# Chunked retention and two MLPs on one core: heads placed by the steps' length, six half tiles under way, value products of two heads in alternation

## Chip, core and metric

One core of a Trainium2 chip runs the whole program. The metric is the device time of one execution in microseconds (us). Three runs of the kernel before gave 1224.64, 1226.80 and 1226.89 us; their median is 1226.8 us.

## The reference, cut to what matters

Queries, keys and values are (4 batches, 8 heads, 768 positions, 64) in f32. A retention layer keeps a 64 x 64 state per batch and head; its output, laid out as 3072 tokens of 512, goes through two MLPs (512 to 2048 to 512) with different activations.

```python
gamma = 1.0 - 2.0 ** (-5.0 - np.arange(H, dtype=np.float32))
for t in range(S):
    state = gamma[None, :, None, None] * state + np.einsum('bhd,bhe->bhde', k[:, :, t], v[:, :, t])
    y[:, :, t] = scale * np.einsum('bhd,bhde->bhe', q[:, :, t], state)
x = y.transpose(0, 2, 1, 3).reshape(B * S, H * D)
h = x @ w_in;  x = np.maximum(0.01 * h, h) @ w_out          # first MLP
h = np.maximum(x @ w2_in, 0.0);  out = (h * h) @ w2_out     # second MLP
```

## The kernel before

**Retention.** The sequence is cut into chunks of 256, so there are 12 units (chunk, batch), the four batches of a chunk in a row. A unit has four pairs of heads; a pair's two heads lie in partitions 0 to 63 and 64 to 127. That makes 48 pairs, numbered 0 to 47 in this order, and 96 heads. For a head, `scores` multiplies keys by queries into PSUM (two blocks: the causal lower part of a 256 x 256 matrix), `soften` multiplies by the mask table on VectorE (L186, the mask product), and `values` multiplies by the values. After the second head of a pair, `outer` updates the state (L231) and `combine` writes the pair's part of the token matrix. `prep_pair` scales queries and values by decay tables first (L121, L122).

The first four units (`WHOLE = 4`, pairs 0 to 15) have no earlier state and are computed in plain f32: these are the unsplit pairs. Their scores contract over 64 partitions (L168, L169), and their value products write 64 output partitions, of the upper or lower half by head (L202, L203). An f32 product appears in the trace as two records. All later heads, the split ones, run as sums of products of f32r operands (a high part and a remainder): L176, L209, L215, with more work for VectorE and ScalarE (L135 to L159, L191, L192, L259, L260).

**MLPs.** The 3072 tokens are six blocks of 512; layer and block give 12 values of n, each with 16 steps, one per 128 columns of the hidden dimension. A step's first half (`emit_in`, L376 or L386) gives the hidden columns in one PSUM bank, `activate` applies the activation (L400, L401), and its second half (`emit_out`, L423 or L446) adds to four accumulator banks. Block 0 of the first layer is cut further: its first `HS = 5` steps take only the first 256 tokens, in plain f32, so that they can start when unit 0 alone is done; eleven steps of full length follow, then the five missing halves:

```python
steps += [(0, j, 0, C) for j in range(HS)]
steps += [(0, j, 0, T) for j in range(HS, NJ)]
steps += [(0, j, C, T) for j in range(HS)]
```

So steps 0 to 4 and 16 to 20 have half the length, steps 5 to 15 the full one, and from step 21 (n = 1) on all are full. From step 5 on weights, activations and tokens are split in f32r parts (`split_w`, L348, L349; `split_x`, L362 to L365).

**Weights** come from memory as 512 KB half tiles, in an 8-byte format that ScalarE and VectorE turn into f32 (`convert`, L303 to L309; VectorE's part is three instructions). `load_half` issues the transfer of the next one, and `convert` calls it again for each half tile used up, so the number under way stays what the start set: three, and one more after the first conversion. Up to step 13 the first layer's weights are converted, two steps ahead of their use (`AHEAD`); the second layer's come from step 80 on (`conv2`).

**Order.** The main loop runs over the steps: the next step's first half, then the heads that `place` put at this step (`head_at`), then this step's second half, then conversions. `place(k)` gives the step for head 8 + k; heads 0 to 7 stand before the loop. Before, heads 8 to 15 all stand at step 0, heads 16 to 31 spread over steps 0 to 13, and then one head stands at each of the steps 14 to 77. The code's order is not that of the engines: when the program is built, a planner orders each engine's instructions by the code's order and by modelled times. `keep_in_program_order` pins an instruction behind the one traced before it on its engine.

PSUM has eight banks: four for the accumulators, three for tag "h" (scores, hidden columns, outer products), one for the values' result y. All loads are issued on SyncE (SP) in one queue.

Of the kernel before, what the change touches and what calls it, by code (L numbers as in the profile page):

```python
# [9 lines left out]
F32 = mybir.dt.float32  # L10
# [7 lines left out]
P = 128  # L18
C = 256
# [23 lines left out]
def retention_then_two_mlps(  # L43
# [150 lines left out]
    def values(hu):  # L194
        u, p, h = hu
        if h == 0:
            y_ps[u, p] = ps_a.tile([P, 2, C], F32, tag="y", name="y")
        if u < WHOLE:
            qs, k, vs = prep[u, p]
            pm = p_sb.pop(hu)  # L200
            y = y_ps[u, p][64 * h:64 * h + 64, 0]
            nc.tensor.matmul(out=y, lhsT=vs[:, 0, h], rhs=pm[:, 128:384], start=True, stop=False)  # L202
            nc.tensor.matmul(out=y[:, P:2 * P], lhsT=vs[:, 1, h], rhs=pm[:, 0:128], start=False, stop=True)  # L203
            return
        q2, kh, kl, v2, vs, w2 = prep[u, p]
        y = y_ps[u, p][:, h]
        start = True
        if w2 is not None:
            nc.tensor.matmul(out=y, lhsT=w2[:, h].rearrange("p a e -> p (a e)"), rhs=q2[h], start=True, stop=False)  # L209
            start = False  # L210
        t = p_sb.pop(hu)
        for n in range(2):
            for sb in range(2):
                c, o = (P, 0) if sb else (0, P)
                nc.tensor.matmul(  # L215
                    out=y[:, c:C], lhsT=v2[:, sb, h].rearrange("p a e -> p (a e)"), rhs=t[:, n, o:o + C - c],
                    start=start, stop=n == 1 and sb == 1,
                )
                start = False

    def outer(up):

# [45 lines left out]
    def load_half():  # L268
        m = n_loaded[0]
        if m < len(halves):  # L270
            lay, j, half = halves[m]
            if lay == 0 and half == 0:
                early_stage[0] = slot(4 + j % 2, [P, 2, DM], U64, "sg")
            if lay == 0:
                t = early_stage[0][:, half]
            elif m % 3 == 2:
                t = a_p.tile([P, DM], U64, tag="r", name="sg", bufs=1)
            else:
                t = stage_p.tile([P, DM], U64, tag="sg", name="sg")
            stage[m] = t  # L280
            nc.sync.dma_start(out=t, in_=w[lay, j, half])
            n_loaded[0] += 1
# [184 lines left out]
    def place(k):  # L467

        if k < 8:
            return k * (HS - LEAD + 1) // 8  # L470
        k -= 8
        a, b = max(HS - LEAD + 1, 0), last_step[0] - LEAD
        if k < 16:
            return a + k * (b - a) // 16
        return b + (k - 16)

    def loads_to(n):
        while n_pairs[0] < min(n, len(ups)):
# [30 lines left out]
                outer(hu[:2])  # L509
            combine(hu[:2])  # L510

    nc.sync.dma_start(out=vt, in_=vtab)
    loads_to(1)
    nc.sync.dma_start(out=qt[:, 0], in_=qtab[:, 0])
    nc.sync.dma_start(out=mk, in_=mask)
    loads_to(2)
    nc.sync.dma_start(out=qt[:, 1:4], in_=qtab[:, 1:4])
    nc.sync.dma_start(out=gt, in_=gtab)
    loads_to(4)
    load_half()  # L520
    load_half()
    load_half()
    first_acc = ps_acc.tile([P, 4, T], F32, tag="acc", name="first_acc")
    for k in range(8):
        hu = hus[k]
        preps_to(k // 2 + 1)
        scores(hu)
        soften(hu)
        values(hu)
        after(hu)  # L530
    loads_to(6)
    need_x(0)
    converted_to(1)
# [9 lines left out]
    for i in range(N):  # L543
# [4 lines left out]
            activate(i + 1)  # L548
        for hu in head_at.get(i, []):
            preps_to(ups.index(hu[:2]) + 1)  # L550
            scores(hu)
            soften(hu)
            values(hu)
            after(hu)
            loads_to(n_prep[0] + 1)
        if i + 1 < N:
# [79 lines left out]
```

## Time and profile before

| | |
|---|---|
| median of three runs | 1226.8 us |
| the profiled execution | 1227.78 us |
| its span in the profile | 1225.8 us |
| TensorE (PE) busy | 1197.4 us, 98% |
| VectorE (DVE) busy | 864.8 us, 71% |
| ScalarE (ACT) busy | 694.8 us, 57% |
| mean granted TensorE clock | 0.995 |
| first matmul starts | 5.50 us |

A busy share is the time in which an engine had an instruction under way; a matmul's record is longer than its turn on the array, as the next one starts before it ends, so turns are read from one start to the next. The chain of work that ended last lies to 90% on TensorE.

### The profile page before, as it was taken

Reading aid. Unit: us, or ns where it says so; the run is one execution under the profiler, and the core shown is the slowest. Engines: PE = TensorE matmul, PEld = TensorE weight load, DVE = VectorE, ACT = ScalarE, POOL = GpSimd, SP = SyncE. Lnnn points to the kernel's source line nnn. Section 1 sums busy time; section 2 is a strip of 40 time slices with the busy share of each in tenths; the row PEclk is TensorE's granted clock in tenths of the full one; section 3 lists DMA queues with packets and bytes.
Section 4 is the critical chain, followed back from the end, with each engine's and each line's share of the span. In section 5 each row is a group of like instructions: output and inputs, shape, how many; then the busy total and the mean of one; then the engine's idle time right before and its main releaser. Section 6 shows DMA issues by size and latency. Waiting matters only on the chain.

```text
span 1225.8 us, 15223 instructions
## 1 busy us (share of the span) xinstructions
PE 1197.4 (98%) x5660; PEld 984.1 (80%) x5660; DVE 864.8 (71%) x1621; ACT 694.8 (57%) x1382; POOL 0.2 (0%) x4
## 2 busy tenths in 40 slices
PE   6799989999999999999999999999999999999998
PEld 4577788888888888888888788888888888888886
DVE  5888589889888888986699955645645555555553
ACT  4666476667666776775477744544534444444443
POOL 0000000000000000000000000000000000000000
PEclk9999999999999999999999999999999999999999
DMA  8664011111111111111045300000000000000000
GB/s 311 232 223 159 18 47 48 58 43 49 60 35 35 45 43 35 41 46 35 18 145 175 128 1 1 35 1 1 35 1 1 35 1 1 35 1 1 35 1 34
DMA packets 22825, 68.81 MB, mean 56 GB/s; under 512 B 2784, under 2 KB 5088, under 8 KB 22752
## 3 DMA queue, kind: packets, MB, share of 16 engines
q1 hardware_dynamic: 22752, 67.85, 16.6%
q8 instruction: 44, 0.72, 0.2%
q14 instruction: 29, 0.24, 0.1%
HBM read 61.55 MB, written 6.29 MB: 55 GB/s over the span
## 4 chain that ended last, share of the span: by engine, by line
PE 90%; DMA 4%; DVE 3%; ACT 2%; issue 1%; SPq 0%; ACTq 0%; DVEq 0%
PE acc L446 40%; PE h L386 40%; DMA sg<-w 3%; PE sc L176 2%; PE y L215 2%; PE y L202 1%; PE sp L231 1%; PE h L376 1%; PE y L209 1%; PE sc L169 1%; PE sc L168 1%; PE acc L423 1%; ACT w L303 1%; DMA gt<-gtab 1%; DVE w L309 0%
## 5 line engine op out<-in xcount | busy, mean ns | idle before, releaser
L386 PE MATMUL h<-xh,wih 128*128 128x512 f32 (+1 forms) x768 | 300.3, 391 | 0.2 <-DVE g L401 0.2
L386 PE MATMUL h<-xl,wih 128*128 128x512 f32 (+1 forms) x768 | 297.8, 388 | 0.9 <-DVE xl L365 0.9
L386 PE MATMUL h<-xh,wil 128*128 128x512 f32 (+1 forms) x768 | 298.5, 389 | 0.0
L349 DVE TENSOR_TENSOR wol<-w,woh 128x512 fp32r<-128x512 f32 x192 | 132.4, 690 | 145.5 <-ACT woh L348 144.4
L348 ACT CAST woh<-w 128x512 fp32r<-128x512 f32 x192 | 119.6, 623 | 181.0 <-PE acc L446 180.0
L386 PEld LDWEIGHTS h<-xl,wih 128*128 128x128 f32 x768 | 144.5, 188 | 30.9 <-DVE xl L365 1.7
L386 PEld LDWEIGHTS h<-xh,wih 128*128 128x128 f32 x768 | 144.5, 188 | 30.7 <-issue 1.2
L386 PEld LDWEIGHTS h<-xh,wil 128*128 128x128 f32 x768 | 144.6, 188 | 29.2 <-DVE wil L349 1.7
L411 DVE TENSOR_TENSOR gl<-g,gh 128x512 fp32r<-128x512 f32 (+1 forms) x192 | 130.8, 681 | 27.9 <-PE acc L446 12.6
L410 ACT CAST gh<-g 128x512 fp32r<-128x512 f32 (+1 forms) x192 | 118.4, 616 | 46.9 <-DVE g L404 26.8
L349 DVE TENSOR_TENSOR wil<-w,wih 128x512 fp32r<-128x512 f32 x192 | 131.4, 684 | 7.4 <-ACT wih L348 7.1
L348 ACT CAST wih<-w 128x512 fp32r<-128x512 f32 x192 | 118.0, 615 | 16.9 <-PE h L386 16.5
L446 PE MATMUL acc<-gh,woh 128*128 128x512 f32 (+1 forms) x388 | 108.8, 393 | 0.0
L404 DVE SCALAR_TENSOR_TENSOR g<-h,g 128x512 f32<-128x512 f32 x96 | 66.3, 690 | 58.8 <-ACT g L403 57.9
L446 PE MATMUL acc<-gh,wol 128*128 128x512 f32 (+1 forms) x388 | 106.2, 385 | 0.0
L446 PE MATMUL acc<-gl,woh 128*128 128x512 f32 (+1 forms) x388 | 105.7, 384 | 0.0
L446 PE MATMUL acc<-woh,gh 128*128 128x512 f32 x384 | 105.6, 389 | 0.0
L446 PE MATMUL acc<-woh,gl 128*128 128x512 f32 x384 | 105.6, 389 | 0.0
L446 PE MATMUL acc<-wol,gh 128*128 128x512 f32 x384 | 105.6, 389 | 0.0
L403 ACT ACTIVATE g<-h 128x512 f32<-128x512 f32 x96 | 57.4, 598 | 72.7 <-PE h L386 67.9
L400 ACT ACTIVATE g<-h 128x512 f32<-128x512 f32 (+1 forms) x101 | 58.0, 574 | 51.6 <-PE h L386 43.0
L446 PEld LDWEIGHTS acc<-woh,gh 128*128 128x128 f32 x384 | 72.1, 188 | 15.0
(83 smaller groups left out, 1515.2 us busy)
## 6 DMA issues: line engine op xcount, KB each, us to landing
sg<-w SPq DMA_DIRECT2D x64, 512.0 KB, 3.8
r<-attn SPq DMA_DIRECT2D x32, 512.0 KB, 3.5
re<-first SPq DMA_DIRECT2D x12, 512.0 KB, 4.9
out<-os SPq DMA_DIRECT2D x24, 256.0 KB, 2.0
kn<-attn SPq DMA_DIRECT2D x16, 128.0 KB, 2.1
r<-first SPq DMA_DIRECT2D x3, 512.0 KB, 5.6
r<-first SPq DMA_DIRECT2D x2, 256.0 KB, 3.2
qt<-qtab SPq DMA_DIRECT2D x1, 384.0 KB, 6.8
```

The costliest lines, as they stand in the source:

```text
L168: nc.tensor.matmul(out=sc[:, 128:256], lhsT=k[a, P:2 * P], rhs=qs[a, P:2 * P], start=True, stop=True)
L176: nc.tensor.matmul(out=sc[:, o:o + C - c], lhsT=kk[:, h * C + sb * P:h * C + (sb + 1) * P], rhs=q2[h][:, c:C], start=n == 0, stop=n == 1,)
L215: nc.tensor.matmul(out=y[:, c:C], lhsT=v2[:, sb, h].rearrange("p a e -> p (a e)"), rhs=t[:, n, o:o + C - c], start=start, stop=n == 1 and ...
L348: nc.scalar.copy(hi, src)
L349: nc.vector.tensor_tensor(out=lo, in0=src, in1=hi.bitcast(F32), op=ALU.subtract)
L386: nc.tensor.matmul(out=hp[:, :c1 - c0], lhsT=a[:, kb * P:(kb + 1) * P], rhs=b[:, c0:c1], start=kb == 0 and k == 0, stop=kb == KB - 1 and k ...
L400: nc.scalar.activation(out=g[:, :m], in_=hp[:, :m], func=AF.Copy, scale=LEAK)
L403: nc.scalar.activation(out=g[:, :m], in_=hp[:, :m], func=AF.Relu)
L404: nc.vector.scalar_tensor_tensor(out=g[:, :m], in0=hp[:, :m], scalar=0.0, in1=g[:, :m], op0=ALU.max, op1=ALU.mult)
L410: nc.scalar.copy(gh[:, :m], g[:, :m])
L411: nc.vector.tensor_tensor(out=gl[:, :m], in0=g[:, :m], in1=gh[:, :m].bitcast(F32), op=ALU.subtract)
L446: nc.tensor.matmul(out=o, lhsT=lhsT, rhs=rhs, start=start and k == 0, stop=stop and k == 2)
```

## The change

Four things change.

- Tables: vt, the first quarter of qt, gt, the mask and the rest of qt are issued on ScalarE's queue instead of SP's, gt and mask earlier among them; the pairs' loads and five half tiles (before: three) stand alone on SP. With the one added by the first conversion, six half tiles are under way. Two of three columns of the first layer take their buffers where they did, the third from the pool that the second layer uses.
- Unsplit pairs run through a new function, `whole_pair`: both heads' scores, both mask products, then the four value products pinned in the order second head, first head, second head, first head.
- Placement: pairs 4 to 7 at steps 0 to 3, pairs 8 to 15 over the full steps 5 to 14, then split heads at steps 15, 17 and 19 and one at each of the steps 21 to 81. Before, seven split heads stood at steps 14 to 20, now three; four heads move to steps 78 to 81.
- In the main loop an unsplit pair runs as a whole at its second head's step.

```diff
--- before.py
+++ after.py
@@ -195,13 +195,6 @@
         u, p, h = hu
         if h == 0:
             y_ps[u, p] = ps_a.tile([P, 2, C], F32, tag="y", name="y")
-        if u < WHOLE:
-            qs, k, vs = prep[u, p]
-            pm = p_sb.pop(hu)
-            y = y_ps[u, p][64 * h:64 * h + 64, 0]
-            nc.tensor.matmul(out=y, lhsT=vs[:, 0, h], rhs=pm[:, 128:384], start=True, stop=False)
-            nc.tensor.matmul(out=y[:, P:2 * P], lhsT=vs[:, 1, h], rhs=pm[:, 0:128], start=False, stop=True)
-            return
         q2, kh, kl, v2, vs, w2 = prep[u, p]
         y = y_ps[u, p][:, h]
         start = True
@@ -217,6 +210,25 @@
                     start=start, stop=n == 1 and sb == 1,
                 )
                 start = False
+
+    def whole_pair(up):
+
+        u, p = up
+        vs = prep[up][2]
+        for h in range(2):
+            scores((u, p, h))
+        for h in range(2):
+            soften((u, p, h))
+        pm = [p_sb.pop((u, p, h)) for h in range(2)]
+        y = y_ps[up] = ps_a.tile([P, 2, C], F32, tag="y", name="y")
+
+        for sb in range(2):
+            c, o = (P, 0) if sb else (0, P)
+            for h in (1, 0):
+                tc.keep_in_program_order(nc.tensor.matmul(
+                    out=y[64 * h:64 * h + 64, 0, c:C], lhsT=vs[:, sb, h], rhs=pm[h][:, o:o + C - c],
+                    start=sb == 0, stop=sb == 1,
+                ))
 
     def outer(up):
 
@@ -269,10 +281,12 @@
         m = n_loaded[0]
         if m < len(halves):
             lay, j, half = halves[m]
-            if lay == 0 and half == 0:
-                early_stage[0] = slot(4 + j % 2, [P, 2, DM], U64, "sg")
-            if lay == 0:
+            if lay == 0 and half == 0 and j % 3 < 2:
+                early_stage[0] = slot(4 + j % 3, [P, 2, DM], U64, "sg")
+            if lay == 0 and j % 3 < 2:
                 t = early_stage[0][:, half]
+            elif lay == 0:
+                t = stage_p.tile([P, DM], U64, tag="sg", name="sg")
             elif m % 3 == 2:
                 t = a_p.tile([P, DM], U64, tag="r", name="sg", bufs=1)
             else:
@@ -467,12 +481,14 @@
     def place(k):
 
         if k < 8:
-            return k * (HS - LEAD + 1) // 8
+            return k * (HS - 1) // 8
         k -= 8
-        a, b = max(HS - LEAD + 1, 0), last_step[0] - LEAD
         if k < 16:
-            return a + k * (b - a) // 16
-        return b + (k - 16)
+            return HS + k * (NJ - 1 - HS) // 16
+        k -= 16
+
+        m = (HS + 1) // 2
+        return NJ - 1 + 2 * k if k < m else first_step[1] + k - m
 
     def loads_to(n):
         while n_pairs[0] < min(n, len(ups)):
@@ -509,25 +525,20 @@
                 outer(hu[:2])
             combine(hu[:2])
 
-    nc.sync.dma_start(out=vt, in_=vtab)
+    nc.scalar.dma_start(out=vt, in_=vtab)
+    nc.scalar.dma_start(out=qt[:, 0], in_=qtab[:, 0])
+    nc.scalar.dma_start(out=gt, in_=gtab)
+    nc.scalar.dma_start(out=mk, in_=mask)
     loads_to(1)
-    nc.sync.dma_start(out=qt[:, 0], in_=qtab[:, 0])
-    nc.sync.dma_start(out=mk, in_=mask)
-    loads_to(2)
-    nc.sync.dma_start(out=qt[:, 1:4], in_=qtab[:, 1:4])
-    nc.sync.dma_start(out=gt, in_=gtab)
+    nc.scalar.dma_start(out=qt[:, 1:4], in_=qtab[:, 1:4])
     loads_to(4)
-    load_half()
-    load_half()
-    load_half()
+    for _ in range(5):
+        load_half()
     first_acc = ps_acc.tile([P, 4, T], F32, tag="acc", name="first_acc")
-    for k in range(8):
-        hu = hus[k]
-        preps_to(k // 2 + 1)
-        scores(hu)
-        soften(hu)
-        values(hu)
-        after(hu)
+    for k in range(NP):
+        preps_to(k + 1)
+        whole_pair(ups[k])
+        after(hus[2 * k + 1])
     loads_to(6)
     need_x(0)
     converted_to(1)
@@ -548,9 +559,14 @@
             activate(i + 1)
         for hu in head_at.get(i, []):
             preps_to(ups.index(hu[:2]) + 1)
-            scores(hu)
-            soften(hu)
-            values(hu)
+            if hu[0] >= WHOLE:
+                scores(hu)
+                soften(hu)
+                values(hu)
+            elif hu[2] == 1:
+                whole_pair(hu[:2])
+            else:
+                continue
             after(hu)
             loads_to(n_prep[0] + 1)
         if i + 1 < N:
```

## Rows read from the trace of the kernel before

**Rows 1.** The page: busy time, share of the span and instructions of each engine.

```profile
PE 1197.4 (98%) x5660; PEld 984.1 (80%) x5660; DVE 864.8 (71%) x1621; ACT 694.8 (57%) x1382; POOL 0.2 (0%) x4
```

**Rows 2.** Busy time by stretch (us, length, engines' busy us, clock, DMA).

```profile
5.00:20.00 15.00, 11.86 (x53) 7.48 (x53) 5.93 (x15) 7.10 (x17) 0.00 (x0) 1.00 0.99 378
20.00:57.00 37.00, 28.73 (x157) 18.73 (x158) 33.01 (x70) 22.42 (x48) 0.00 (x0) 0.99 0.70 245
...
57.00:120.00 63.00, 63.00 (x297) 47.13 (x297) 56.30 (x110) 44.80 (x86) 0.00 (x0) 0.98 0.60 204
...
150.00:200.00 50.00, 44.79 (x284) 40.36 (x283) 44.38 (x101) 34.77 (x82) 0.00 (x0) 0.93 0.16 49
...
560.00:600.00 40.00, 40.00 (x188) 33.43 (x187) 23.68 (x40) 20.08 (x37) 0.00 (x0) 1.00 0.04 14
```

**Rows 3.** TensorE's timeline (start us, us, what, xrecords) around values and scores.

```profile
17.93 0.97 PE L202 MATMUL y<-pm,vs 128*64 128x256 f32 x4
...
19.04 0.50 PE L168 MATMUL sc<-qs,re 64*128 64x128 f32 x4
...
19.90 0.71 PE L231 MATMUL first_acc<-vs,re 128*128 128x128 f32 x4
...
75.59 0.65 PE L202 MATMUL y<-pm,vs 128*64 128x256 f32 x2
...
76.39 0.48 PE L168 MATMUL sc<-qs,re 64*128 64x128 f32 x2
...
77.24 0.71 PE L231 MATMUL sp<-vs,re 128*128 128x128 f32 x4
...
98.55 0.50 PE L168 MATMUL sc<-qs,r 64*128 64x128 f32 x4
```

**Rows 4.** Groups of TensorE, 57 to 150.4 us (xrecords, busy us, mean ns, idle before).

```profile
L202 PE MATMUL y<-pm,vs 128*64 128x256 f32 x30 | 9.7, 404 | 0.0
```

**Rows 5.** Timeline of the start, SP, ScalarE and VectorE; then the DMA issue.

```profile
3.99 0.43 SPq L518 DMA_DIRECT2D gt<-gtab  x1
10.57 1.28 ACT L239 ACT_TABLE_LOAD   x1 [10.57 <-DMA gt<-gtab]
12.81 0.22 DVE L156 TENSOR_TENSOR w<-state,w 64x64 fp32r<-64x64 f32 x1 [2.60 <-ACT w L153]
...
gt<-gtab SPq DMA_DIRECT2D x1, 2.0 KB, 6.5
```

**Rows 6.** Groups of VectorE over the span, forms apart (xcount, busy us, mean ns).

```profile
L186 DVE TENSOR_TENSOR pm<-sc,mk 128x384 f32<-128x384 f32 x96 | 53.2, 555 | 23.7 <-PE sc L176 15.0 <-PE sc L169 7.8
L192 DVE TENSOR_TENSOR ph<-pm,ph 128x384 fp32r<-128x384 f32 x64 | 35.2, 550 | 0.2
L142 DVE TENSOR_TENSOR q<-qs,q 64x256 fp32r<-64x256 f32 x64 | 26.9, 420 | 7.8 <-ACT q L139 3.8
L136 DVE TENSOR_TENSOR kl<-r,kh 128x512 fp32r<-128x512 f32 x32 | 21.9, 685 | 0.0
L122 DVE TENSOR_TENSOR vs<-r,vt 128x256 f32<-128x256 f32 x36 | 15.1, 420 | 8.6 <-DMA r<-first 5.0 <-PE y L203 1.9 <-DMA r<-attn 1.4
```

**Rows 7.** TensorE's timeline in the half steps ([idle before, releaser]).

```profile
177.82 0.33 PE L176 MATMUL sc<-q,kh 128*128 128x128 f32 x1 [1.41 <-DVE pm L186]
...
181.22 1.22 PE L231 MATMUL sp<-vs,kn 128*128 128x128 f32 x4 [2.69 <-DVE g L401]
182.10 1.20 PE L446 MATMUL acc<-gh,woh 128*128 128x256 f32 x4
```

**Rows 8.** Waits of the span: us in total, times, longest us.

```profile
ACT w L303 <- DMA sg<-w: 27.9, 29, 2.8
...
PE y L202 <- DVE pm L186: 8.2, 7, 2.3
```

**Rows 9.** TensorE's timeline: the same eight records after a pause, and later.

```profile
56.58 3.44 PE L376 MATMUL h<-xs,w 128*128 128x256 f32 x8
...
67.44 1.89 PE L376 MATMUL h<-xs,w 128*128 128x256 f32 x8
```

## Prediction

> **What bounds the kernel now.** I read the page's busy shares first, then the same shares stage by stage, then the TensorE timeline of the two stages that are not dense, then who waited for whom. TensorE is busy for 98% of the span [rows 1], so most of the run can only be shortened by giving TensorE less to do. The stages differ, though. Between 5 and 57 us TensorE and VectorE both have gaps: VectorE fills 5.9 of 15 us while the first data come in, and then 33 of 37 us, so from 20 us on VectorE is the fuller engine. From 57 to 120 us TensorE is full, and VectorE is at 56.3 of 63 us: only 6.7 us of it are free. From 150 to 200 us TensorE has 5.2 us of idle time and VectorE is at 44.4 of 50 us: that is the stretch of the half-length steps with split heads between them. At 560 to 600 us TensorE is full and VectorE at 23.7 of 40 us [rows 2]. After 700 us nothing in the change is executed.
>
> The profiled execution took 1227.78 us around a span of 1225.8 us; the median of the runs is 1226.8 us. I sum against 1227.8 and take 1 us off at the end.
>
> **A, tables on the ScalarE queue.** The 2 KB table gt was issued at 3.99 us, as the eighth DMA of the one queue, and took 6.5 us to land. ScalarE stood until 10.57 us for it, and VectorE idled 2.60 us for what ScalarE makes with it [rows 5]; the second head's mask product stands behind that in VectorE's order, and that head's value products behind the mask product. Issued third on a queue of its own it should land before the first outer product is done. Worth between 0 (pair 1's data, not gt, is the last to come) and 3 us; I take 2.5, near the idle time in the row. The five issues move to ScalarE, which has nothing to do until 10.57 us, so they cost nothing; if that cover went, five issues of some 0.4 us would cost 2.
>
> Against this speaks a rule of the Trainium skill ("DMA: Bandwidth & Descriptors", Issuing engines are not separate DMA queues): transfers started by different engines share the same 16 DMA engines and interleave. The trace has those engines at a 0.99 share between 5 and 20 us [rows 2], which agrees. By the rule alone A would be only the issue slot ahead of the first pair, some 0.4 us, and the forecast would be 1211.
>
> **B, value products of both heads together.** One head alone holds TensorE from 75.59 to 76.39 us, 0.80 us, so a pair takes 1.60. Once the trace shows both heads' value products issued back to back with both inputs ready (four records, then the next work starts): 17.93 to 19.04 us, 1.11 us for the pair, although its first half still runs at half the later speed. The two heads write different 64 columns of the array and run at the same time [rows 3]. At full speed I estimate 0.85 for the pair, from that row and the single head's 0.80: 0.75 saved. Between 57 and 150.4 us there are 30 records of the first value product, two to a head, so 15 heads or 7.5 pairs [rows 4], with TensorE full: 7.5 x 0.75 = 5.6 us. The bounds are half of it (2.8, if every other pair is still broken up) and all of it. In 20 to 57 us I count nothing, as VectorE is the fuller engine there. The wait that this adds: all four products of a pair now stand behind the second head's mask product, where the first head's could go earlier. Behind them on TensorE stand the outer product and the next step's products, and whatever reads those. TensorE waited for mask products 7 times before, 8.2 us in all, 2.3 at most [rows 8].
>
> **C, scores of both heads together.** The same overlap exists already for scores: 0.86 us for a pair at 19.04 us (x4 records) against 0.85 for one head at 76.39 us [rows 3]. In the full stretch only the pair at 98.55 us has it; the other six pairs had their heads placed in different steps. Now every pair's scores are issued from one call. Each needs two of the three PSUM buffers of the tag, which the step's own product also uses, so not all will meet. From 0 to 6 x 0.84 = 5.0 us; I take four pairs, 3.4, because the one pair whose two heads shared a late step did meet.
>
> **D, heads respread, six half tiles.** Until step 5 eight pairs are due instead of eleven. A pair costs VectorE two mask products of 0.555 and two preparations of 0.42 us, 1.95 in all [rows 6]: three pairs are 5.9 us that leave the stretch in which VectorE is the fuller engine, and return in steps 5 to 14. Two more half tiles on the way help where ScalarE waits for weights (27.9 us over the whole run, at most 2.8 at once) [rows 8], but VectorE was nearly full meanwhile. Each half tile is 512 KB, about 1.4 us at the 378 GB/s of the start [rows 2], and two more of them stand ahead of pairs 4 and 5 in SP's queue. Their data have until the fourth pair is done, so 0, or +2.8 without that cover. Range -5.9 to +2.8; I take -2, nearer to the unused time of VectorE (4 us in 20 to 57).
>
> **E, split heads off the half steps.** Steps 14 to 20 held seven split heads, now three. The stretch 150 to 200 us lost 5.2 us of idle time [rows 2], above all 1.41 for a mask product and 2.69 for a step's activation; and behind that pause four 256-column products at 182.10 us last 1.20 us [rows 7], with the mean granted clock of the stretch at 0.93 [rows 2], so at the lower of its two levels (1.2 and 2.4 GHz) for a while. I estimate that slowdown at 2.4 us: the row's group and the dozen products behind it at double time. One split head costs VectorE at least 0.555 + 0.550, and half of its pair's 0.685 + 4 x 0.42: 2.3 us [rows 6]. Four fewer are 9 us out of 44.4 in a stage of some 38: no longer the fuller engine. TensorE's part of these heads only moves to steps 78 to 81, where TensorE was full anyway and VectorE has 16 of 40 us free [rows 2], which covers 9; without that cover it would cost what E brings. Their loads end later on SP, one step ahead of the second layer's first weights, whose third buffer they share; I put that at 0, or +2 if SP stands there for a step's preparation. E: -4 (only the two named pauses) to -10; I take 5.2 + 2.4 = -7.6.
>
> **F, what VectorE takes back.** In 57 to 120 us five pairs lie. B and C would cut 5 x (0.75 + 0.56) = 6.6 us there, all of the 6.7 that VectorE has free [rows 2], and with D's three pairs it gets more. It will not reach 100%. Between 0 and +6.6; I take +3.5, the middle.
>
> **Sum.** -2.5 - 5.6 - 3.4 - 2.0 - 7.6 + 3.5 = -17.6 us: 1227.8 becomes 1210.2, and 1209 as a median.
>
> **Rivals.**
> R1, VectorE takes all of it early: F eats B, C and D, and A and E stay. 1227.8 - 2.5 - 7.6 = 1217.7, so 1217. For it: 56.3 of 63 us in the full stretch [rows 2]. Against: part of that fullness is work done ahead. The clock makes a second form of it, R2: TensorE, relieved, pauses more often in 20 to 120 us, and a pause is followed by slow products, as at 56.58 us, where eight took 3.44 us against 1.89 later [rows 9]. Four more such spots are +6.2: 1215. The Trainium skill ("TensorE: Matmul & The Clock Gate", Why this matters for your kernels) has it as a rule that a pause between bursts of matmuls drops the clock to half; the row agrees.
> R3, more: VectorE keeps up (F at 0), C and D near their ends, E at -9: 2.5 + 5.6 + 5 + 5 + 9 = 27, 1200.
> R4, slower: the pinned order. If TensorE stands at each of the 12 pairs from the fifth on for the second mask product, at 2.3 us, the longest such wait now [rows 8], that is +27.6 against A to E's 21.1: 1227.8 + 6.5 - 1, 1233. It decides from 21.1 / 12 = 1.8 us a pair; the mean of the 7 waits is 1.2, and 25 of 32 heads had none.
> R5, the change doesn't do what it says: the order within each engine is set by a planner, and if other products come between, or the heads do not overlap, B and C are gone, but F with them: A + D + E = -12, 1215.
>
> **Chances.** Forecast (1204 to 1214) 0.45; R1 0.17; R2 0.07; R3 0.15; R4 0.08; R5 0.08. 1199 to 1220 holds all but R4, the far end of R3 and the weak end of R1. A measurement of this kernel tells about 0.2% (2.5 us) from no change. Faster: all but R4 and an end of R1 and R5, 0.87; same 0.05; slower 0.08.
>
> **What would show it.** A: ScalarE's first work well before 10 us, no 2.6 us gap on VectorE. B and C: x4 records of the value and score lines throughout, at 0.85 us a pair. D: the first split product (L386's line) at 63 to 70 us instead of 72.5. E: TensorE idle and granted clock between steps 15 and 21: under 2 us, 1.0. F: VectorE above 93% until the conversions end. Wrong would be: waits for mask products over 15 us in all (R4), singles among the value records (R5), or a new gap of TensorE after 560 us, from the later heads.

## The result, and the profile after

| | before | after |
|---|---|---|
| median | 1226.85 us | 1216.13 us (1215.32 to 1216.74) |
| profiled execution, span | 1227.78, 1225.8 us | 1216.53, 1214.5 us |
| mean granted clock | 0.995 | 0.993 |

The ratio is 0.9912, with a 95% interval from 0.9900 to 0.9923: 10.7 us less, where the prediction had 17.8 less. So the sign was right and the time was 7 us off: it lies inside the wide range that was given (1199 to 1220) and 2 us above the narrow one that was held likeliest (1204 to 1214).

In the code of after, the value products of the unsplit pairs have the line L228, the outer product L243, the split heads L176, L202 and L208, a step's first half L390 (unsplit) and L400 (split), its second half L437 and L460, and the conversions L317 to L323. Scores and mask products kept L168, L169 and L186.

The busy line of the page of after, in answer to [rows 1]:

```profile
PE 1187.4 (98%) x5660; PEld 977.7 (81%) x5660; DVE 863.0 (71%) x1621; ACT 691.8 (57%) x1382; POOL 0.2 (0%) x4
```

As many instructions on every engine, and TensorE busy for 10.0 us less. Busy times by stretch of after, in answer to [rows 2] (us, length, busy us of the five engines, granted clock, DMA share, GB/s):

```profile
5.00:20.00 15.00, 12.10 (x56) 7.93 (x56) 9.21 (x22) 10.63 (x23) 0.00 (x0) 1.00 1.02 397
20.00:57.00 37.00, 29.91 (x151) 21.22 (x149) 34.55 (x73) 24.31 (x50) 0.00 (x0) 0.86 0.74 261
57.00:100.00 43.00, 38.82 (x188) 28.36 (x187) 41.38 (x82) 29.68 (x57) 0.00 (x0) 0.96 0.59 214
150.00:200.00 50.00, 49.71 (x310) 43.75 (x310) 45.18 (x100) 35.78 (x82) 0.00 (x0) 1.00 0.17 51
560.00:600.00 40.00, 40.00 (x193) 33.60 (x192) 32.38 (x61) 24.48 (x50) 0.00 (x0) 1.00 0.10 33
```

The stretch from 57 to 100 us in the kernel before:

```profile
57.00:100.00 43.00, 43.00 (x207) 32.23 (x207) 38.88 (x77) 31.05 (x59) 0.00 (x0) 0.97 0.67 225
```

Four things are to be seen. Between the half steps (150 to 200 us) TensorE is full and the clock at 1.00: of the 5.2 us of idle time 0.3 are left. At 560 to 600 us VectorE has taken the later heads (23.7 to 32.4 us) and TensorE does not notice. But from 57 to 100 us the roles are exchanged: TensorE, full before, has 4.2 us of idle time, and VectorE is at 41.4 of 43 us. And between 20 and 57 us the granted clock fell from 0.99 to 0.86.

TensorE's timeline of after (start us, us, what, xrecords, [idle before, releaser]):

```profile
22.77 1.07 PE L228 MATMUL y<-pm,vs 128*64 128x256 f32 x8 [2.50 <-DVE pm L186]
23.78 0.81 PE L168 MATMUL sc<-qs,re 64*128 64x128 f32 x4
...
25.37 3.50 PE L390 MATMUL h<-xs,w 128*128 128x256 f32 x12
...
63.00 0.50 PE L400 MATMUL h<-xh,wih 128*128 128x512 f32 x1
...
82.60 0.87 PE L228 MATMUL y<-pm,vs 128*64 128x256 f32 x8
83.40 1.22 PE L460 MATMUL acc<-gl,woh 128*128 128x256 f32 x8
...
85.48 0.50 PE L168 MATMUL sc<-qs,re 64*128 64x128 f32 x4
```

A pair's value products are now one group of eight records and take 0.80 us from start to start (82.60 to 83.40), as long as one head alone took [rows 3]. At 22.77 us stands the price: 2.50 us of waiting for the mask product, and then slow work at the lower of the clock's two levels (the granted clock from 24 to 26 us is 0.50; the scores at 23.78 us take 0.81 us, the same four records at 85.48 us 0.50). The first split product starts at 63.00 us, before at 72.55.

Waits in after, in answer to [rows 8] (us in total, times, longest):

```profile
PE y L228 <- DVE pm L186: 4.8, 6, 2.5
...
ACT w L317 <- DMA sg<-w: 29.2, 25, 2.6
```

**Work and loss.** Busy shares hide the clock, so I set each of the 5660 matmul records of a trace, from its start to the next one's, against the shortest turn its shape has in the dense stretches (0.227 us for 512 columns, 0.216 for one f32 record of 256); records that run beside a partner count with what they took. The sum of the shortest turns is the work, the rest is loss, by waiting or by a slow clock. First start, work and loss add up to the span.

| us | first start | work | loss to step 5 | steps 5 to 14 | step 15 and the half steps, to 200 or 210 us | later |
|---|---|---|---|---|---|---|
| before | 5.5 | 1149.0 | 25.8 | 7.4 | 12.0 | 26.2 |
| values_alone | 5.2 | 1138.2 | 28.6 | 6.5 | 14.1 | 26.7 |
| u_place | 5.3 | 1137.9 | 37.8 | 8.3 | 11.7 | 26.6 |
| split_only | 5.2 | 1137.7 | 38.2 | 8.5 | 5.1 | 27.5 |
| u_order | 5.4 | 1149.9 | 18.7 | 13.1 | 7.2 | 27.1 |
| after | 5.2 | 1138.3 | 26.0 | 12.5 | 4.8 | 27.6 |
| no_shift | 5.1 | 1137.8 | 21.5 | 10.2 | 5.2 | 27.3 |

Before to after: work -10.7, half steps -7.2, and 5.1 us lost anew in steps 5 to 14, 1.4 later. The span fell by 11.3. The kernels between the two are the experiments.

### The profile page after: what moved, and what is told of

It is laid out like the page before. It is cut to its first block, busy times and chain, and to the rows that moved or that the text cites. A ratio compares the mean times of both kernels' runs of the same rounds, so it can differ in the third digit from the quotient of the medians.

```text
span 1214.5 us, 15223 instructions
## 1 busy us (share of the span) xinstructions
PE 1187.4 (98%) x5660; PEld 977.7 (81%) x5660; DVE 863.0 (71%) x1621; ACT 691.8 (57%) x1382; POOL 0.2 (0%) x4
## 4 chain that ended last, share of the span: by engine, by line
PE 83%; DVE 10%; DMA 4%; ACT 2%; issue 1%; ACTq 0%; SPq 0%; DVEq 0%
PE acc L460 38%; PE h L400 37%; DMA sg<-w 3%; PE sc L176 2%; PE y L208 2%; DVE w L320 2%; DVE w L323 2%; DVE wil L363 1%; PE sp L243 1%; DVE w L319 1%; PE y L202 1%; DVE pm L186 1%; DVE g L415 1%; DVE wol L363 1%; DVE gl L425 1%
## 5 line engine op out<-in xcount | busy, mean ns | idle before, releaser
L400 PE MATMUL h<-xh,wih 128*128 128x512 f32 (+1 forms) x768 | 300.4, 391 | 2.8 <-DVE g L415 1.2
L400 PE MATMUL h<-xh,wil 128*128 128x512 f32 (+1 forms) x768 | 298.2, 388 | 0.0
L400 PE MATMUL h<-xl,wih 128*128 128x512 f32 (+1 forms) x768 | 297.9, 388 | 0.1
L400 PEld LDWEIGHTS h<-xh,wih 128*128 128x128 f32 x768 | 144.5, 188 | 33.4 <-DVE g L415 2.5
L400 PEld LDWEIGHTS h<-xl,wih 128*128 128x128 f32 x768 | 144.3, 188 | 30.3 <-issue 1.0
L400 PEld LDWEIGHTS h<-xh,wil 128*128 128x128 f32 x768 | 144.5, 188 | 28.7 <-DVE wil L363 1.3
L460 PE MATMUL acc<-gh,woh 128*128 128x512 f32 (+1 forms) x388 | 109.5, 395 | 2.1 <-ACT gh L424 2.1
L460 PE MATMUL acc<-gh,wol 128*128 128x512 f32 (+1 forms) x388 | 106.2, 386 | 0.0
L460 PE MATMUL acc<-gl,woh 128*128 128x512 f32 (+1 forms) x388 | 105.9, 384 | 0.0
L460 PE MATMUL acc<-wol,gh 128*128 128x512 f32 x384 | 105.5, 389 | 0.0
L460 PE MATMUL acc<-woh,gh 128*128 128x512 f32 x384 | 105.5, 389 | 0.0
L460 PE MATMUL acc<-woh,gl 128*128 128x512 f32 x384 | 105.5, 389 | 0.0
L460 PEld LDWEIGHTS acc<-woh,gl 128*128 128x128 f32 x384 | 72.1, 188 | 15.0
```

The lines of the kernel that those rows point to most:

```text
L400: nc.tensor.matmul(out=hp[:, :c1 - c0], lhsT=a[:, kb * P:(kb + 1) * P], rhs=b[:, c0:c1], start=kb == 0 and k == 0, stop=kb == KB - 1 and k ...
L460: nc.tensor.matmul(out=o, lhsT=lhsT, rhs=rhs, start=start and k == 0, stop=stop and k == 2)
```

## The experiments

Ratios are to the kernel before, run on the same chip, with a 95% interval. After stands at 0.9912, and 0.001 is 1.2 us. By the intervals, a difference of two such ratios is uncertain by some 2 us.

**The placement undone (u_place).** After, with the old `place`:

```diff
         if k < 8:
-            return k * (HS - 1) // 8
+            return k * (HS - LEAD + 1) // 8
         k -= 8
+        a, b = max(HS - LEAD + 1, 0), last_step[0] - LEAD
         if k < 16:
-            return HS + k * (NJ - 1 - HS) // 16
-        k -= 16
-
-        m = (HS + 1) // 2
-        return NJ - 1 + 2 * k if k < m else first_step[1] + k - m
+            return a + k * (b - a) // 16
+        return b + (k - 16)
```

> The changed kernel with the heads placed as before (whole pairs at their second head's step). Theory: the respread gives 7.5 us in the half-length steps, taken from idle and slow-clock time of TensorE between 150 and 200 us, so without it some 7 to 8 us come back: 1223 to 1225 us. Rival: the gain is TensorE's relief by the value products of both heads together, and the placement only moves work: 1216 to 1218 us.

Measured: 1230.45 against 1227.76 us, ratio 1.0024 (1.0013 to 1.0035). Both expectations were too low. The placement is worth some 13.5 us within after, and without it the other three parts together make the kernel slower than before. In the table the loss to step 5 is 37.8 instead of 26.0 us.

**Only the split heads moved (split_only).** Unsplit heads placed as before, split heads as in after:

```diff
         if k < 8:
-            return k * (HS - 1) // 8
+            return 0
         k -= 8
         if k < 16:
-            return HS + k * (NJ - 1 - HS) // 16
+            return k * 14 // 16
```

> The changed kernel with the unsplit heads placed as before (pairs 4 to 7 at step 0, pairs 8 to 15 over steps 0 to 13) and the split heads as in the change. Theory: by TensorE's lost time the 13 us that the old placement costs are two parts, some 7 for the unsplit heads (before 150 us) and some 7 for the split ones (150 to 210 us): about 7 us slower than the changed kernel, near 1224. Rival a: the split heads carry all, and this is within 2 us of the changed kernel. Rival b: the unsplit heads carry all, and this is 12 us slower or more.

Measured: 1225.00 against 1226.52 us, 0.9986 (0.9977 to 0.9995). So of the 13.5 us some 5 belong to the split heads (1.0024 to 0.9986) and some 9 to the unsplit ones (0.9986 to 0.9912). The stretch of the half steps in u_place:

```profile
150.00:200.00 50.00, 44.38 (x290) 39.82 (x289) 44.85 (x104) 34.94 (x85) 0.00 (x0) 0.97 0.18 53
```

and in split_only:

```profile
150.00:200.00 50.00, 48.47 (x299) 42.59 (x298) 42.92 (x92) 33.66 (x76) 0.00 (x0) 1.00 0.12 38
```

VectorE is no longer the fuller engine there, and TensorE's idle time falls from 5.6 to 1.5 us.

**Products of both heads together, and nothing else (values_alone).** Before, with `whole_pair` (its text as in the change) and the calls of it; tables, half tiles and placement as before:

```diff
-    for k in range(8):
-        hu = hus[k]
-        preps_to(k // 2 + 1)
-        scores(hu)
-        soften(hu)
-        values(hu)
-        after(hu)
+    for k in range(NP):
+        preps_to(k + 1)
+        whole_pair(ups[k])
+        after(hus[2 * k + 1])
...
-            scores(hu)
-            soften(hu)
-            values(hu)
+            if hu[0] >= WHOLE:
+                scores(hu)
+                soften(hu)
+                values(hu)
+            elif hu[2] == 1:
+                whole_pair(hu[:2])
+            else:
+                continue
```

> The kernel before with only the unsplit pairs' part of the change: both heads' scores, both mask products, then the four value products pinned in alternation, each pair run at its second head's old step. Tables, half tiles and the heads' steps stay as before. Theory: with five pairs at step 0 and nothing else for TensorE in between, TensorE stands for the second mask products while VectorE is full, and the saved 0.8 us a pair are paid back: within 3 us of the kernel before or slower, 1226 to 1230, with waits of the value products for mask products of 11 us or more. Rival, the terms B, C and F of the forecast taken alone (5.6 + 3.4 - 3.5): 1221 to 1222.

Measured: 1220.89 against 1227.76 us, 0.9948 (0.9935 to 0.9961). After u_place I had thought the pair function harmful without the new placement; it is not. By itself it brings 6.4 us of 10.8 (by the ratios), and the rival, which kept to the prediction's steps B, C and F, was right.

So tables and half tiles, which are all that u_place has beyond values_alone, cost some 9 us under the old placement, all of it ahead of step 5 (28.6 to 37.8 in the table). What they do there is seen on VectorE. Its groups from 0 to 50 us in values_alone (xcount, busy us, mean ns, idle before): mask products and the last of the three instructions of a conversion,

```profile
L186 DVE TENSOR_TENSOR pm<-sc,mk 128x384 f32<-128x384 f32 x16 | 8.6, 549 | 1.1 <-PE sc L169 1.1
L328 DVE CUSTOM_DVE_ANT_0 w<-sg,w 128x1024 uint16<-128x1024 uint16 x11 | 7.5, 684 | 0.1
```

and in u_place:

```profile
L323 DVE CUSTOM_DVE_ANT_0 w<-sg,w 128x1024 uint16<-128x1024 uint16 x13 | 8.9, 682 | 0.6 <-ACT sg L318 0.6
L186 DVE TENSOR_TENSOR pm<-sc,mk 128x384 f32<-128x384 f32 x14 | 7.6, 548 | 0.1
```

With weights at hand earlier, VectorE has done two conversions more by 50 us and two mask products fewer. The old placement has the first 16 heads and two more ahead of step 2 in the code, and in both traces step 2 follows some 5.5 us behind the sixteenth mask product. VectorE's timeline of values_alone has that at

```profile
48.89 0.55 DVE L186 TENSOR_TENSOR pm<-sc,mk 128x384 f32<-128x384 f32 x1
```

and TensorE's timeline then

```profile
49.58 1.54 PE L235 MATMUL y<-pm,vs 128*64 128x256 f32 x8 [3.75 <-DVE pm L186]
...
54.10 2.50 PE L395 MATMUL h<-xs,w 128*128 128x256 f32 x5 [0.23 <-DVE pm L186]
```

In u_place the same places are

```profile
58.01 0.55 DVE L186 TENSOR_TENSOR pm<-sc,mk 128x384 f32<-128x384 f32 x1
```

and

```profile
50.67 1.55 PE L228 MATMUL y<-pm,vs 128*64 128x256 f32 x8 [3.24 <-DVE pm L186]
...
58.70 1.55 PE L228 MATMUL y<-pm,vs 128*64 128x256 f32 x8 [3.74 <-ACT w L317]
...
63.76 0.80 PE L390 MATMUL h<-xs,w 128*128 128x256 f32 x1 [0.77 <-DVE pm L186]
```

(the wait at 58.70 us is put down to ScalarE, but the mask product that began at 58.01 us ends last). The sixteenth mask product is 9.1 us later, and step 2 is 9.7 us later. The eight records at 49.58, 50.67 and 58.70 us take 1.5 us, at the clock's lower level, instead of 0.87. Under the new placement step 2 stands behind fewer pairs, so the conversions may go ahead without holding it up; that this is why they cost nothing there is argued from the traces: after has the same 13 of them by 50 us and only 12 mask products, and step 2 starts at 41.3 us. Which of the two, tables or half tiles, moves the conversions under the old placement was not run apart.

**Three half tiles at the start instead of five (u_three).**

```diff
-    for _ in range(5):
+    for _ in range(3):
         load_half()
```

> The changed kernel with three half tiles issued at the start instead of five. Theory: VectorE is full from 20 to 100 us, so earlier weights have little to give: within 1.5 us of 1216. Rival: the six half tiles under way are what brought step 5 forward by 9.5 us: 1220 us or more.

Measured: 1216.76 against 1227.76 us, 0.9914 (0.9899 to 0.9929): no difference to after.

**Tables back on SP's queue (u_tables).**

```diff
-    nc.scalar.dma_start(out=vt, in_=vtab)
-    nc.scalar.dma_start(out=qt[:, 0], in_=qtab[:, 0])
-    nc.scalar.dma_start(out=gt, in_=gtab)
-    nc.scalar.dma_start(out=mk, in_=mask)
+    nc.sync.dma_start(out=vt, in_=vtab)
     loads_to(1)
-    nc.scalar.dma_start(out=qt[:, 1:4], in_=qtab[:, 1:4])
+    nc.sync.dma_start(out=qt[:, 0], in_=qtab[:, 0])
+    nc.sync.dma_start(out=mk, in_=mask)
+    loads_to(2)
+    nc.sync.dma_start(out=qt[:, 1:4], in_=qtab[:, 1:4])
+    nc.sync.dma_start(out=gt, in_=gtab)
     loads_to(4)
```

> The changed kernel with the tables back on SP's queue in their old order. Theory: the gt table again lands 3 us later, VectorE idles 2 to 3 us more in the first 13 us, and since it is full from then to the end of the conversions, the whole is 2.5 us slower: 1218.6. Rival: the loss at the start is covered later, as the sum of TensorE's losses before step 5 was the same in both kernels: 1216.

Measured: 1217.04 against 1227.76 us, 0.9916 (0.9900 to 0.9931): no difference either. The mechanism of step A is there in after, in the timeline of ScalarE's queue, ScalarE and VectorE, against [rows 5]:

```profile
1.64 0.45 ACTq L530 DMA_DIRECT2D gt<-gtab  x1
7.45 1.28 ACT L251 ACT_TABLE_LOAD   x1 [7.45 <-DMA gt<-gtab]
9.69 0.49 DVE L156 TENSOR_TENSOR w<-state,w 64x64 fp32r<-64x64 f32 x2 [2.09 <-ACT w L153]
```

VectorE has the state at 9.69 us instead of 12.81. But step 0 starts at 25.37 us in after and at 24.14 in u_tables: by 25 us VectorE has begun the last instruction of four conversions in after and of two in u_tables, and of six mask products in both, so the 3 us were spent on conversions, not on what TensorE waited for. This run also tells what the slow clock of after is worth. Its stretch from 20 to 57 us has the full clock:

```profile
20.00:57.00 37.00, 30.46 (x172) 21.33 (x168) 37.00 (x79) 27.54 (x56) 0.00 (x0) 1.00 0.81 275
```

Step 5 starts at 59.98 us, 3.0 earlier than in after, but step 16 at 151.07 against 151.77, and the whole takes as long: what TensorE gained early it lost again before step 16, with VectorE busy all the time from 20 to 57 us.

**The value products head by head (u_order), and head by head but pinned (pin_by_head).** The first:

```diff
-        for sb in range(2):
-            c, o = (P, 0) if sb else (0, P)
-            for h in (1, 0):
-                tc.keep_in_program_order(nc.tensor.matmul(
+        for h in range(2):
+            for sb in range(2):
+                c, o = (P, 0) if sb else (0, P)
+                nc.tensor.matmul(
                     out=y[64 * h:64 * h + 64, 0, c:C], lhsT=vs[:, sb, h], rhs=pm[h][:, o:o + C - c],
                     start=sb == 0, stop=sb == 1,
-                ))
+                )
```

> The changed kernel with a pair's four value products head by head and not pinned, both heads' mask products still ahead of them. Theory: that both heads' inputs are ready and the products stand next to each other is what counts, as the one pair of the kernel before that overlapped had the order head by head: value records still in eights at 0.80 us a pair, within 1.5 us of 1216. Rival: the alternation is needed for the overlap: 1.6 us a pair, 4 to 8 us slower, 1220 to 1224.

The second has the loops of u_order and keeps `tc.keep_in_program_order` around each product:

```diff
-        for sb in range(2):
-            c, o = (P, 0) if sb else (0, P)
-            for h in (1, 0):
+        for h in range(2):
+            for sb in range(2):
+                c, o = (P, 0) if sb else (0, P)
                 tc.keep_in_program_order(nc.tensor.matmul(
```

> The changed kernel with a pair's four value products pinned as now, but head by head (first head's two, then the second's) instead of in alternation. Theory: what the fixed order brings is that the planner puts nothing between the two heads; two neighbours overlap in either order, as the scores of a pair do, which stand head by head: value records in eights at 0.80 us a pair and a time within 1.5 us of the changed kernel's. Rival: the alternation itself is needed: value records of a pair take 1.6 us though neighbours, 5 to 8 us slower than the changed kernel.

Measured: u_order 1224.25 against 1227.76 us, 0.9977 (0.9966 to 0.9989); pin_by_head 1224.48 against 1226.52, 0.9980 (0.9970 to 0.9990). Both are some 8 us slower than after. TensorE's timeline of u_order, in the dense stretch:

```profile
75.53 0.86 PE L228 MATMUL y<-pm,vs 128*64 128x256 f32 x4
76.32 0.50 PE L400 MATMUL h<-xh,wih 128*128 128x512 f32 x1
...
84.13 0.86 PE L228 MATMUL y<-pm,vs 128*64 128x256 f32 x4
84.92 0.71 PE L243 MATMUL sp<-vs,re 128*128 128x128 f32 x4
```

and of pin_by_head:

```profile
28.80 0.86 PE L228 MATMUL y<-pm,vs 128*64 128x256 f32 x4
29.59 1.56 PE L390 MATMUL h<-xs,w 128*128 128x256 f32 x6
31.08 0.86 PE L228 MATMUL y<-pm,vs 128*64 128x256 f32 x4
```

Groups of four, 0.79 us each, with other products between. A pin holds the order of what it pins and does not keep other work out. No input was missing there: in pin_by_head the two mask products ended at 26.71 and 27.77 us, before the first group began, and still a step's products stand between the heads, in the order that the planner made. Where nothing stands between, two heads overlap in the order head by head too. The first pair of pin_by_head shows it:

```profile
11.03 2.00 PE L228 MATMUL y<-pm,vs 128*64 128x256 f32 x8 [0.15 <-DVE pm L186]
12.96 0.81 PE L168 MATMUL sc<-qs,re 64*128 64x128 f32 x4
```

Its second mask product ended at 11.44 us, and the second head's first record starts at 11.50, 0.47 us behind the first head's. At the speed of that stretch the pair takes 1.93 us; one head alone took 1.48 (13.71 to 15.19 us in before), and the alternating pair at 11.28 us in after 1.48. So the alternation as such is not what lets heads overlap. It begins with the second head, so the whole pair stands behind the second mask product, and I take it that this leaves the planner no room between the heads; the second head's two products first and then the first head's was not run, so this is argued, not shown. In the table u_order has 11.6 us more work than after, some 9.5 of it in the value products and some 2.5 in the scores, which meet in 8 of 16 pairs there and in 12 in after; 7 to 8 us are seen at the end, mainly because u_order loses 7.3 us less ahead of step 5.

**Less work for VectorE (no_shift, b_no_shift).** One of VectorE's three instructions is left out of the conversions of the first layer, in after and in before:

```diff
-        nc.vector.tensor_scalar(out=ru, in0=ru, scalar1=3, scalar2=None, op0=ALU.logical_shift_left)
+        if lay == 1:
+            nc.vector.tensor_scalar(out=ru, in0=ru, scalar1=3, scalar2=None, op0=ALU.logical_shift_left)
```

> The changed kernel without VectorE's first instruction (the shift) in the conversions of the first layer's weights, so these weights are not what they should be. 32 instructions of 0.42 us, one issued 0.34 after the other, are 11 us of VectorE's 95 before 100 us. Theory: VectorE is the bound until the conversions end, so 7 to 11 us go: 1206 to 1210. Rival: VectorE is full only because it works ahead, and TensorE's pauses come from waits for data and from the slow clock after them: less than 3 us, 1214.

> The kernel before without VectorE's shift in the conversions of the first layer's weights, so these weights are not what they should be; 11 us of VectorE less, as in no_shift. Theory: in the kernel before TensorE was full from 57 us on and VectorE near full only up to there, so the relief is worth less than the 7 us it is worth in the changed kernel: 2 to 5 us, 1222 to 1225. Rival: VectorE bounded both kernels alike: 7 us or more, under 1220.

Measured: no_shift 1209.08 against 1226.52 us, 0.9863 (0.9848 to 0.9877), so some 6 us less than after; b_no_shift 1221.09 against 1227.10, 0.9941 (0.9923 to 0.9959), 6.0 less than before by the medians and 7.2 by the ratio. Some 11 us taken from VectorE are worth 6 to 7 in either kernel. I had expected clearly less in before, where TensorE is full from 57 us on; but VectorE bounds its start too: step 5 of b_no_shift starts at 63.5 us, 9.1 earlier than in before. The stretch from 20 to 57 us of no_shift has TensorE at 32.5 us with the full clock, where after has 29.9 at 0.86 (and of no_shift's gain over after, 4.5 us lie ahead of step 5 in the table and 2.3 in steps 5 to 14):

```profile
20.00:57.00 37.00, 32.53 (x168) 22.86 (x166) 35.44 (x69) 28.67 (x59) 0.00 (x0) 1.00 0.86 325
```

**Preparations on GpSimd (pool_prep).** Queries and values of the unsplit pairs scaled on GpSimd instead of VectorE:

```diff
-        nc.vector.tensor_tensor(out=qs, in0=q, in1=qt[:, p], op=ALU.mult)
-        nc.vector.tensor_tensor(
+        eng = nc.gpsimd if u < WHOLE else nc.vector
+        eng.tensor_tensor(out=qs, in0=q, in1=qt[:, p], op=ALU.mult)
+        eng.tensor_tensor(
```

> The changed kernel with the two preparing products of the unsplit pairs (scaled queries and values) on GpSimd, which is idle, instead of VectorE: 32 instructions of 0.42 us leave VectorE. Theory: VectorE is the bound until 100 us, so up to 11 us go, less what GpSimd's own duration adds ahead of each pair's scores: 1207 to 1213. Rival: GpSimd is so slow, or disturbs VectorE so much, that TensorE waits for the prepared tiles instead: 1216 or more.

Measured: 1216.30 against 1226.52 us, 0.9911 (0.9896 to 0.9926): no gain, although VectorE was relieved of the 32 instructions. GpSimd's groups over the span (xcount, busy us, mean ns, idle before):

```profile
L123 POOL TENSOR_TENSOR vs<-re,vt 128x256 f32<-128x256 f32 x12 | 15.2, 1268 | 54.3 <-PE y L229 25.7 <-DMA re<-first 15.9 <-PE h L401 6.4
L122 POOL TENSOR_TENSOR qs<-re,qt 128x256 f32<-128x256 f32 x12 | 10.3, 856 | 27.8 <-PE sc L170 22.3 <-DMA qt<-qtab 4.3 <-issue 1.1
```

A scaling of 0.42 us on VectorE takes 0.86 to 1.27 here. Each pair needs one of either kind, one after the other, ahead of its scores and outer product. Step 5 starts at 60.45 us, 2.6 earlier than in after, and step 21 at 167.96, 0.4 earlier, so what was gained ahead of step 5 was lost behind it. That the delay of the preparations is what ate it is argued, not shown; longer instructions of VectorE beside GpSimd (last section) are another candidate.

**The later unsplit pairs elsewhere (late_a, late_7_14).** Pairs 8 to 15 at the steps 9, 10, 11, 12, 13, 13, 14, 14 (with their loads issued ahead of their preparation), and at the steps 7 to 14:

```diff
         if k < 16:
-            return HS + k * (NJ - 1 - HS) // 16
+            return (9, 10, 11, 12, 13, 13, 14, 14)[k // 2]
...
         if i + 1 in head_at:
+            loads_to(ups.index(head_at[i + 1][-1][:2]) + 1)
             preps_to(ups.index(head_at[i + 1][-1][:2]) + 1)
```

> The changed kernel with pairs 8 to 15 at steps 9, 10, 11, 12, 13, 13, 14, 14 instead of 5, 6, 8, 9, 10, 11, 13, 14 (and a pair's data loaded ahead of its preparation where two stand at one step). Theory: VectorE is the fuller engine until the conversions end near 100 us, and TensorE after that; about four pairs (1.95 us of VectorE each) leave the first stretch, so the conversions end earlier and 3 to 6 us go: ratio to the kernel before 0.986 to 0.989. Rival: TensorE only gets the pairs later, when it is full, and what VectorE gains in the first stretch TensorE cannot use: within 1.5 us of the changed kernel's 0.991.

```diff
         if k < 16:
-            return HS + k * (NJ - 1 - HS) // 16
+            return 7 + k // 2
```

> The changed kernel with pairs 8 to 15 at steps 7 to 14, one at each, instead of 5, 6, 8, 9, 10, 11, 13, 14. A smaller dose of the same: two pairs leave steps 5 and 6. Theory: 1 to 3 us faster than the changed kernel. Rival: no difference beyond 1 us.

Measured: late_a 1216.81 against 1227.10 us, 0.9911 (0.9889 to 0.9932), no difference; late_7_14 1219.56 against 1227.10, 0.9934 (0.9914 to 0.9953), 2 to 3 us slower by the medians, though the intervals touch. In late_a step 9 starts at 84.4 us, 9.3 us ahead of after, and step 16 at 151.73, after 151.77: the pairs put off must be paid before step 16. Where between step 5 and step 14 they stand moves the loss and does not remove it.

## Why the prediction was right or wrong

**B and C, right in mechanism and in their sum.** 9.0 us were forecast for both; TensorE's work fell by 10.7 and rises by 11.6 when the heads stand apart (u_order). That the sum came so near is partly luck, as each by itself was off and the two misses partly cancel: counted by group, the value products' work fell from 20.3 to 10.9 us (9.4, forecast 5.6, as B counted nothing ahead of 57 us) and the scores' from 15.4 to 13.5 (1.9, forecast 3.4). The pair at 0.85 us was 0.80. All 16 unsplit pairs now have their value products in eights, and the scores of 12 of 16 meet (9 before). With F, the forecast had 5.5 and values_alone measured 6.4 to 6.9.

**E, right in mechanism, somewhat large in size.** Forecast 7.6; the loss of the half steps fell by 7.2, to 4.8 us with the clock at 1.00, while the runs say about 5 (u_place to split_only), so up to 3 us of the miss may lie here. At 560 to 600 us, where the later heads' work landed, TensorE stayed full, as said.

**A, wrong.** Forecast 2.5; u_tables shows no difference beyond its interval. The bound "between 0 and 3" held, but I took the upper part because that idle time stood in the row. The state did come 3 us earlier; what I did not ask was which work would fill the time gained. It went to conversions, and VectorE was the fuller engine until 100 us anyway. The rule of the Trainium skill that I weighed against A ("DMA: Bandwidth & Descriptors", Issuing engines are not separate DMA queues) has a second issuing engine save no more than issue time; that gave 0.4 for A, which is nearer. The trace agrees: of the 3.1 us by which the small table came sooner, 2.35 are its earlier issue (1.64 instead of 3.99 us).

**D, wrong as a term of its own.** Forecast 2.0. Its sign came as announced: step 5 starts at 63.00 us instead of 72.55. But that is because the work of three pairs and more moved behind it; the loss to step 5 is 26.0 against 25.8 us. Worse, D was set down as independent of the rest, and it is not: six half tiles and tables cost some 9 us with the old placement (values_alone to u_place) and nothing, each undone alone, with the new one (u_three, u_tables), and the new placement of the unsplit heads gains some 9 us where these are present (split_only to after). The two nearly cancel. By these ratios the pair function and the split heads' new steps alone would give some 11 us (6.4 and 4.7), all that the change brought; that kernel was not run. ScalarE's waits for weights, which the half tiles were to shorten, came to 29.2 us in after against 27.9 [rows 8]. My "+2.8 without that cover" looked for the price in SP's queue; it lay in VectorE's order, where a tile that is there earlier is converted earlier, ahead of mask products.

**F, near in size, and wrong in place and cause.** I took 3.5 between 0 and 6.6, for what VectorE would take back of B and C from 57 to 120 us, since it "will not reach 100%". In values_alone, where only B's and C's cause is changed, 10.8 us less work brought 6.4, so some 4 were taken back; but they lie ahead of step 5 (2.8 more lost) and in the half steps (2.1), and steps 5 to 14 lose 0.9 less than before. In after VectorE is at 41.4 of 43 us from 57 to 100 us, over the 93% named, and steps 5 to 14 lose 5.1 us more. That loss goes with the new placement and not with B and C: u_order has it (13.1 us) with its value products apart, and values_alone (6.5) and split_only (8.5), which have B and C and the old placement, have not. So D's pairs, which the prediction let return in steps 5 to 14 without a price of their own, were paid for there. Why TensorE pauses there is open in part: in no_shift VectorE is relieved, and steps 5 to 14 still lose 10.2 of 12.5 us.

**The sum by stages.** Forecast B + C + E: -16.6; measured -10.7 - 7.2 = -17.9. Forecast A + D + F: -1.0; measured +6.4 (loss to step 5 +0.2, steps 5 to 14 +5.1, later +1.4, first start 0.3 earlier). By stages the error lies in the second group. The runs put it in A and D, together nothing where 4.5 were forecast, and in E, about 5 for 7.6; B, C and F together gave 6.4 for 5.5.

**The rivals.** R1 gave 1217, which is nearest, but not for its reason: it had VectorE eat B, C and D whole and A stay, and values_alone kept 6.4 us of B and C while A brought nothing. R2's clock was seen: 0.86 from 20 to 57 us, and behind the pause of 2.50 us at 22.77 us twelve records take 3.50 us. The Trainium skill ("TensorE: Matmul & The Clock Gate", Why this matters for your kernels) has a pause between bursts of matmuls lower the clock; that row agrees. As the reason for the missing 7 us it fails, as u_tables has the full clock there and takes as long; in u_place, at 0.77 from 20 to 57 us, no run takes it apart from the waiting. R4 did not come: value products waited 4.8 us for mask products, less than the 8.2 before, since for 10 of 16 pairs the second mask product was ready too; with scores and outer products that waited for one it was 8.8 us in all, well under the 15 named. R5 became true only in u_order and pin_by_head, and then as "other products come between", not as "the heads do not overlap". R3 had its B, C and E, and lacked a VectorE that keeps up.

## What to carry to other kernels

When a change takes work off an engine in a stretch where another is nearly full, charge the gain against the second engine's free time first, and look for the payment in every stretch where that engine is full, not only in the one that was relieved. Work that is moved out of a full stretch has a price where it is put, and belongs in the sum with it. Of each transfer or table that will come earlier, ask what its reader does with the time: a busy engine may start work that is not urgent ahead of work that is. And let parts be costed together when they meet in one engine's order: here two of them cost 9 us with one placement and nothing with another.

## What the runs showed of the hardware

Products that write different 64 output columns of the array run fully beside each other where both have their inputs and nothing stands between them: 0.80 us for two heads, 0.80 for one (75.59 to 76.39 in [rows 3], 82.60 to 83.40 in after). [rows 3] had suggested 0.85.

After a pause of 2.5 to 3.8 us the same eight records took 1.07 to 1.55 us instead of 0.87 (granted clock 0.50 from 24 to 26 us in after, and from 49.5 to 51 us in values_alone), and of the kernels above the slowest, u_place, had the lowest clock over the whole span, 0.985.

By its records GpSimd took 0.81 to 1.27 us for the 128 x 256 scaling that VectorE does in 0.42. While it worked, some instructions of VectorE were longer than in after: from 20 to 100 us the remainder of the tokens (128 x 512) took 813 ns on average instead of 686, one of the weights' 772 instead of 685; the other remainder of the weights did not change (682 and 687). The Trainium skill ("GPSIMD Engine Reference", Key points) states that the two engines share their SBUF interfaces and contend where a VectorE instruction reads two SBUF inputs, as these two do; the longer times agree, and no run isolates the cause.
